# k and v loads over all 128 partitions, q halves on two queues, and the first batch's attention chain reordered with its last ninth deferred, in a linear attention + MLP kernel

## The chip, the cores and the metric

The kernel runs on one core of one Trainium2 chip. The metric is the time of one execution on the device in microseconds (us). Executions of one kernel mostly agree within 0.3 to 1%; where an execution was marked as slow (over 1.5% above the fastest of the same kernel), it is left out. The span of the profile is about 1.8 us shorter than the timed execution.

## The reference

```python
# q, k, v: [8 batches, 8 heads, 576 tokens, 64], float32
q_s = softmax(q, over the 64 columns)
k_s = softmax(k, over the 576 tokens)
kv  = einsum('bhsd,bhse->bhde', k_s, v)          # 64 x 64 per head
out = einsum('bhsd,bhde->bhse', q_s, kv)
x   = out with heads side by side                # 4608 tokens x 512
h   = x @ w_in                                   # 512 -> 2048
g   = max(0.01 * h, h)
return g @ w_out                                 # 2048 -> 512, float32
```

The work is dominated by the two products of the MLP: 9 tiles of 512 tokens, each with 64 matmuls of 128x512 for GEMM1 (`ph`) and 64 for GEMM2 (`pout`). One batch has 576 tokens, so a batch of attention gives one whole tile of 512 tokens and its last ninth (64 tokens) goes into the next tile.

## The kernel before

All of q, k and v arrive as halves of 64 partitions: one transfer for partitions 0 to 63, one for 64 to 127. A partition holds 9 consecutive tokens of a head, so each piece is 2304 bytes. Each half is 590 KB.

```python
def load(eng, dst, src_dram, b, nm, half):
    if nm == "q":
        src = src_dram[b, half * NG : (half + 1) * NG, :, :]      # heads 0-3 | 4-7
    else:
        src = src_dram[b].rearrange("(g hp) s d -> hp g s d", hp=2)[half]   # even | odd heads
    eng.dma_start(out=dst[half * HP : (half + 1) * HP, :, :],
                  in_=src.rearrange("h (p r) d -> p h (r d)", r=R))
...
for nm in "qkv":
    emit_load(nc.sync, states[0], 0, nm)          # first batch: six halves on SP's queue
...
# GpSimd's queue. The copy waits for the first batch's k: it holds back all that follows.
nc.gpsimd.tensor_copy(out=gate[HP:P, :], in_=states[0]["k"][HP:P, NG - 1, 0:1])
for i in range(WQ):
    emit_w_in(i)                                  # four quarters of w_in, cast to bf16 on the way
emit_load(nc.gpsimd, states[1], 1, "q")
emit_w_out(0)
emit_w_out(1)
emit_load(nc.gpsimd, states[1], 1, "k")
emit_w_out(2)
emit_load(nc.gpsimd, states[1], 1, "v")
emit_w_out(3)
for nm in "qkv":
    emit_load(nc.gpsimd, states[2], 2, nm)
```

The first batch's attention runs before the first tile of the MLP. `dummies` are matmuls with zero weights whose result nobody uses; they are there to keep TensorE's clock up. In the kernel before they also read the exponentials of q and k, so the first of them starts at 13.04 us. In the changed kernel they read the zero tile alone and start at 1.19 us.

```python
def first_attn(st):
    make_qexp(st, b, 0)(); make_qexp(st, b, 1)()      # ScalarE
    make_kexp(st, b, 0)(); make_kexp(st, b, 1)()      # ScalarE, one call per half
    make_qnorm(st, b, 0)()                            # VectorE: sum, reciprocal, multiply
    dummies(7, ...)
    make_transpose(st, b, [0], 0, R - 1, nc.scalar.copy)()
    make_qnorm(st, b, 1)()
    dummies(6, ...)
    make_vcast(st, b, 0, 2)(); make_vcast(st, b, 2, NG)()
    make_transpose(st, b, [1], 0, R - 1)()
    dummies(4, ...)
    make_kv(st, b, 0, 2)(); make_kv(st, b, 2, NG)()
    make_transpose(st, b, [0, 1], R - 1, R)()         # the last ninth
    for g in range(NG):
        make_out(st, b, g, copies[g % 2])()           # 512 and 64 tokens
```

During GEMM2 of the first tile (the loop runs over j = 0 to 15 outside, so w_out is needed quarter by quarter), the second batch's attention is prepared in slots: its k at j = 5, transposes at 6 to 8, v at 10, kv products at 12.

The softmax here doesn't subtract the row's maximum and nothing guards it: scores larger than these inputs give would overflow.

Of the kernel before, what the change touches and what calls it, by code (L numbers as in the profile page):

```python
# [18 lines left out]
def kernel(  # L19
# [50 lines left out]
    def load(eng, dst, src_dram, b, nm, half):  # L70
        if nm == "q":
            src = src_dram[b, half * NG : (half + 1) * NG, :, :]
        else:
            src = src_dram[b].rearrange("(g hp) s d -> hp g s d", hp=2)[half]
        eng.dma_start(  # L75
            out=dst[half * HP : (half + 1) * HP, :, :],
            in_=src.rearrange("h (p r) d -> p h (r d)", r=R),
        )

    dram = {"q": q, "k": k, "v": v}  # L80

    def emit_load(eng, st, b, nm):
        st[nm] = ld_pool.tile([P, NG, R * D], FP32, name=f"{nm}_ld", tag="ld")
        for half in range(2):
            load(eng, st[nm], dram[nm], b, nm, half)

    states = {b: {} for b in range(B)}
    for nm in "qkv":
        emit_load(nc.sync, states[0], 0, nm)
# [9 lines left out]
    for i in range(2):  # L99
# [4 lines left out]
        nc.vector.memset(ke[0:HP, :, :, HP:P], 0.0)  # L104
        nc.vector.memset(ke[HP:P, :, :, 0:HP], 0.0)
        nc.vector.memset(vb[:, :, :, D:VW], 1.0)
        nc.vector.memset(kd, 0.0)
# [3 lines left out]
        kd_buf.append(kd)  # L111

# [22 lines left out]
    nc.gpsimd.tensor_copy(out=gate[HP:P, :], in_=states[0]["k"][HP:P, NG - 1, 0:1])  # L135
    for i in range(WQ):
        emit_w_in(i)
    emit_load(nc.gpsimd, states[1], 1, "q")
    emit_w_out(0)
    emit_w_out(1)  # L140
    emit_load(nc.gpsimd, states[1], 1, "k")
    emit_w_out(2)
    emit_load(nc.gpsimd, states[1], 1, "v")
    emit_w_out(3)
    for nm in "qkv":
        emit_load(nc.gpsimd, states[2], 2, nm)
# [3 lines left out]
    def dummies(n, rhs):  # L150
        if "t" not in scratch:
            scratch["t"] = ps_pool.tile([P, TT], FP32, name="scr", tag=BANK)
        for _ in range(n):
            nc.tensor.matmul(scratch["t"], lhsT=wsrc[:, 0:P], rhs=rhs, start=True, stop=True)  # L154

    def flat(ap):
        return ap.rearrange("p a b -> p (a b)")
# [11 lines left out]
    def make_kexp(st, b, hp):  # L169
        def piece():  # L170
            lo = hp * HP
            nc.scalar.activation(  # L172
                out=ke_buf[b % 2][lo : lo + HP, :, :, lo : lo + HP],
                in_=st["k"][lo : lo + HP, :, :].rearrange("p g (r d) -> p g r d", d=D),
                func=AF.Exp,
            )

        return piece
# [10 lines left out]
    def make_qnorm(st, b, gl):  # L189
        def piece():  # L190
            x = qe_buf[b % 2][:, gl, :, :].rearrange("p r (h d) -> p (r h) d", d=D)
            qsum = small_pool.tile([P, 2 * R], FP32, name="qsum")
            qrec = small_pool.tile([P, 2 * R], FP32, name="qrec")
            nc.vector.reduce_sum(out=qsum, in_=x, axis=AX.X)  # L194
            nc.vector.reciprocal(out=qrec, in_=qsum)
# [3 lines left out]
                in1=qrec.unsqueeze(2).to_broadcast([P, 2 * R, D]),  # L199
# [64 lines left out]
    def make_out(st, b, g, big=None):  # L264
        def piece():
            t, o = divmod(b * S, TT)
            n1 = TT - o
            for c0, c1, tt, oo in ((0, n1, t, o), (n1, S, t + 1, 0)):
                po = ps_pool.tile([P, c1 - c0], FP32, name="po", tag=BANK)
# [3 lines left out]
                copy = nc.scalar.copy if c0 == 0 else nc.vector.tensor_copy  # L273
                if c0 == 0 and big is not None:
                    copy = big
                copy(out=xT_of(tt)[:, g, oo : oo + c1 - c0], in_=po)  # L276
# [3 lines left out]
    def prep_pieces(b, st):  # L280
# [5 lines left out]
            make_kexp(st, b, 0),  # L286
            make_kexp(st, b, 1),
# [11 lines left out]
    def out_pieces(b, st, copies=None):  # L299
        return [make_out(st, b, g, copies) for g in range(NG)]  # L300

    def first_attn(st):
        b = 0
        qe, ke = qe_buf[0], ke_buf[0]
        copies = (nc.scalar.copy, nc.vector.tensor_copy)
# [172 lines left out]
```

## Time and profile before

| | before |
|---|---|
| time, median (lowest to highest of 3) | 310.95 us (308.95 to 311.01) |
| span of the profile | 309.0 us |
| first matmul of GEMM1 | 24.42 us |
| first matmul of GEMM2, first tile | 38.23 us |
| first matmul of GEMM1, second tile | 63.59 us |
| from there to the end | 245.4 us |

From the second tile on, PE is busy nearly all the time. What can be won lies in the first 64 us.

The page cuts the span into 40 slices of 7.7 us; digits are busy tenths, PEclk is the granted TensorE clock in tenths. DMA and GB/s show what the 16 DMA engines did.

```profile
PE   0379994899999999999999999999999999999993
...
PEclk9999999599999999999999999999999999999998
DMA  7999999996996981699169917981400220121022
GB/s 163 222 211 224 222 225 224 226 234 172 221 210 164 224 176 34 160 217 185 34 159 220 188 34 160 224 178 34 105 0 2 68 68 0 36 68 34 2 68 68
```

The DMA engines are full from the start to about 60 us (the first eight slices), yet move only some 220 GB/s. PE is nearly idle in the first two slices, and the clock drops to half in one slice.

The next lines are from the timeline of the kernel before: start in us, duration, engine, source line, operation, output<-inputs, shapes, and in brackets how long the engine had been idle and what ended it.

```profile
8.74 2.21 ACT L161 ACTIVATE qe_102<-q_ld 128x1152 bf16<-128x1152 f32 x2 [6.50 <-DMA q_ld<-in_q_dram]
...
14.10 0.18 POOL L135 COPY gate<-k_ld 64x1 f32<-64x1 f32 x1 [12.79 <-DMA k_ld<-in_k_dram]
...
19.51 1.72 DVE L182 CAST vb_104<-v_ld 128x1152 bf16<-128x1152 f32 x2 [3.57 <-DMA v_ld<-in_v_dram]
...
24.42 13.98 PE L326 MATMUL ph<-xT,w_in_sb 128*128 128x512 bf16 x64
```

ScalarE waits 6.5 us for q, VectorE waits 3.6 us for v, GpSimd lets the weights go only at 14.1 us, and GEMM1 starts 4.9 us after v's cast begins. The times of the loads from issue to landing give 5.8 and 8.6 us for q, 11.3 and 14.0 for k, 16.6 and 19.4 for v: one half every 2.7 us, which is 590 KB / 2.7 us = 218 GB/s.

The second loss is in GEMM2 of the first tile (timeline of the kernel before, PE):

```profile
47.81 1.02 PE L335 MATMUL pout<-w_out_sb,g_sb 128*128 128x512 bf16 x4 [1.61 <-DMA w_out_sb<-in_moe_w_out_dram]
...
55.34 1.87 PE L335 MATMUL pout<-w_out_sb,g_sb 128*128 128x512 bf16 x4 [3.81 <-DMA w_out_sb<-in_moe_w_out_dram]
```

PE waits 1.6 and 3.8 us for quarters of w_out, and after the second wait four matmuls take 1.87 us instead of 1.02: this is the half clock.

### The profile page before, as it was taken

The numbers are of one execution on the slowest core, as the hardware profiler recorded it, in microseconds if no ns is written. First come the engines' busy times: TensorE is split into PE (matmuls) and PEld (weight loads), VectorE is DVE, ScalarE is ACT, GpSimd is POOL, SyncE is SP. The second block draws the span as 40 slices with busy tenths as digits, with TensorE's granted clock in tenths as the row PEclk, the third lists the DMA queues.
The fourth block names the chain that finished last, engine by engine and source line by source line (L and its number), as shares of the span: only waits on it lengthen the run. The fifth ranks groups of instructions, "written<-read, shape, count | busy, mean of one in ns | idle before, by whom it ended". The sixth has DMA issues, their size and how long they took to land.

```text
span 309.0 us, 4094 instructions
## 1 busy us (share of the span) xinstructions
PE 283.3 (92%) x1665; PEld 138.8 (45%) x1665; DVE 131.9 (43%) x235; ACT 142.4 (46%) x189; POOL 14.7 (5%) x27
## 2 busy tenths in 40 slices
PE   0379994899999999999999999999999999999993
PEld 0144452444545544554455445544544444444441
DVE  6653082337795609460946094609460100110021
ACT  1725761079663484358435833583343046006400
POOL 0171321000000000000000000000000000000000
PEclk9999999599999999999999999999999999999998
DMA  7999999996996981699169917981400220121022
GB/s 163 222 211 224 222 225 224 226 234 172 221 210 164 224 176 34 160 217 185 34 159 220 188 34 160 224 178 34 105 0 2 68 68 0 36 68 34 2 68 68
DMA packets 21522, 42.21 MB, mean 137 GB/s; under 512 B 2048, under 2 KB 6144, under 8 KB 21504
## 3 DMA queue, kind: packets, MB, share of 16 engines
q1 hardware_dynamic: 15552, 30.68, 45.3%
q0 software_dynamic: 5952, 11.27, 18.4%
q8 instruction: 13, 0.21, 0.3%
q14 instruction: 5, 0.04, 0.0%
HBM read 36.70 MB, written 9.44 MB: 149 GB/s over the span
## 4 chain that ended last, share of the span: by engine, by line
PE 78%; DMA 15%; ACT 2%; POOL 1%; issue 1%; SPq 1%; DVE 0%; POOLq 0%
PE pout L335 38%; PE ph L326 34%; DMA w_out_sb<-in_moe_w_out_dram 6%; DMA q_ld<-in_q_dram 6%; DMA k_ld<-in_k_dram 4%; PE pkv L238 3%; PE po L270 2%; PE pt L213 2%; ACT ke_103 L172 1%; POOL w_in_sb L123 1%; ACT g_sb L356 1%; SPq L75 1%; DVE out_sb L345 0%; POOL q_ld L75 0%; POOL gate L135 0%
## 5 line engine op out<-in xcount | busy, mean ns | idle before, releaser
L356 ACT ACTIVATE g_sb<-ph 128x512 bf16<-128x512 f32 x144 | 84.4, 597 | 111.7 <-PE ph L326 109.3
L335 PE MATMUL pout<-w_out_sb,g_sb 128*128 128x512 bf16 x576 | 129.1, 382 | 5.5 <-DMA w_out_sb<-in_moe_w_out_dram 5.4
L326 PE MATMUL ph<-xT,w_in_sb 128*128 128x512 bf16 x576 | 132.9, 379 | 0.0
L335 PEld LDWEIGHTS <-g_sb 128*128 128x128 bf16 x576 | 56.3, 98 | 72.4 <-issue 7.1
L326 PEld LDWEIGHTS <-w_in_sb 128*128 128x128 bf16 x576 | 54.9, 98 | 58.9 <-issue 0.2
L345 DVE COPY out_sb<-pout 128x512 f32<-128x512 f32 x36 | 24.3, 688 | 111.4 <-PE pout L335 104.8
L276 DVE CAST xT<-po 128x64 bf16<-128x64 f32 (+7 forms) x54 | 21.0, 425 | 7.1 <-PE po L270 6.5
L222 DVE COPY qT<-pt 128x128 bf16<-128x128 bf16 (+1 forms) x31 | 13.0, 447 | 14.2 <-PE pt L213 14.2
L172 ACT ACTIVATE ke_111<-k_ld 64x2304 bf16<-64x2304 f32 x8 | 16.9, 2118 | 2.7 <-DMA k_ld<-in_k_dram 2.7
L172 ACT ACTIVATE ke_103<-k_ld 64x2304 bf16<-64x2304 f32 x8 | 16.9, 2116 | 1.0 <-DMA k_ld<-in_k_dram 0.9
L194 DVE TENSOR_REDUCE qsum<-qe_110 128x18 f32<-128x1152 bf16 x8 | 10.8, 1350 | 13.7 <-ACT qe_110 L161 13.6
L276 ACT CAST xT<-po 128x448 bf16<-128x448 f32 (+2 forms) x10 | 4.8, 524 | 22.9 <-PE po L270 22.9
L154 PE MATMUL scr<-qe_102,wsrc 128*128 128x512 bf16 x7 | 3.2, 631 | 13.0 <-DVE qe_102 L196 13.0
L194 DVE TENSOR_REDUCE qsum<-qe_102 128x18 f32<-128x1152 bf16 x8 | 10.8, 1349 | 3.0 <-ACT qe_102 L161 2.9
L161 ACT ACTIVATE qe_102<-q_ld 128x1152 bf16<-128x1152 f32 x8 | 9.0, 1156 | 6.6 <-DMA q_ld<-in_q_dram 6.5
L196 DVE TENSOR_TENSOR qe_102<-qe_102,qrec 128x1152 bf16<-128x1152 bf16 x8 | 10.9, 1358 | 0.3
L196 DVE TENSOR_TENSOR qe_110<-qe_110,qrec 128x1152 bf16<-128x1152 bf16 x8 | 10.9, 1358 | 0.3
L161 ACT ACTIVATE qe_110<-q_ld 128x1152 bf16<-128x1152 f32 x8 | 9.0, 1155 | 2.1 <-DMA q_ld<-in_q_dram 2.0
L154 PEld LDWEIGHTS <-wsrc 128*128 128x128 bf16 x17 | 1.8, 115 | 15.1 <-DVE qe_102 L196 13.0
L246 DVE RECIPROCAL krec<-pkv 128x2 f32<-128x2 f32 x16 | 2.7, 169 | 12.6 <-PE pkv L238 12.5
L182 DVE CAST vb_104<-v_ld 128x2304 bf16<-128x2304 f32 (+1 forms) x5 | 5.8, 1171 | 3.6 <-DMA v_ld<-in_v_dram 3.6
L238 PEld LDWEIGHTS <-ke_111 128*128 128x128 bf16 x144 | 6.4, 107 | 2.0 <-issue 0.6
(40 smaller groups left out, 102.3 us busy)
## 6 DMA issues: line engine op xcount, KB each, us to landing
out_dram<-out_sb SPq DMA_DIRECT2D x72, 128.0 KB, 2.3
q_ld<-in_q_dram SPq DMA_DIRECT2D x12, 576.0 KB, 6.4
k_ld<-in_k_dram SPq DMA_DIRECT2D x12, 576.0 KB, 10.2
v_ld<-in_v_dram SPq DMA_DIRECT2D x12, 576.0 KB, 14.4
q_ld<-in_q_dram POOLq DMA_DIRECT2D x4, 576.0 KB, 18.6
k_ld<-in_k_dram POOLq DMA_DIRECT2D x4, 576.0 KB, 21.0
v_ld<-in_v_dram POOLq DMA_DIRECT2D x4, 576.0 KB, 20.0
w_in_sb<-in_moe_w_in_dram POOLq DMA_DIRECT2D x4, 512.0 KB, 9.4
```

Of the source, the lines that this page charges most:

```text
L161: nc.scalar.activation(out=qe_buf[b % 2][:, gl, :, :].rearrange("p r (h d) -> p h r d", d=D), in_=st["q"][:, 2 * gl : 2 * gl + 2, :].rearr ...
L172: nc.scalar.activation(out=ke_buf[b % 2][lo : lo + HP, :, :, lo : lo + HP], in_=st["k"][lo : lo + HP, :, :].rearrange("p g (r d) -> p g r ...
L194: nc.vector.reduce_sum(out=qsum, in_=x, axis=AX.X)
L196: nc.vector.tensor_tensor(out=x, in0=x, in1=qrec.unsqueeze(2).to_broadcast([P, 2 * R, D]), op=ALU.mult,)
L213: nc.tensor.matmul(pt[:, i, r - r0, :], lhsT=qe_buf[b % 2][:, gl, r, :], rhs=ident, is_transpose=True, start=(i == 0 and r == r0), stop=(i ...
L222: (copy or nc.vector.tensor_copy)(out=st["qT"][:, gl::2, r0 * HP : r1 * HP].rearrange("c gh (r p) -> c r gh p", p=HP), in_=pt[:, i, :, :]. ...
L238: nc.tensor.matmul(pkv[:, g - g0, 0 : D + 1], lhsT=ke[:, g, r, :], rhs=vb[:, g, r, 0 : D + 1], start=(r == 0), stop=(r == R - 1),)
L276: copy(out=xT_of(tt)[:, g, oo : oo + c1 - c0], in_=po)
L326: nc.tensor.matmul(ph, lhsT=w_in_sb[:, cb, j * P : (j + 1) * P], rhs=x[:, cb, :], start=(cb == 0), stop=(cb == NB - 1),)
L335: nc.tensor.matmul(pout, lhsT=g_sb[:, j, tsub * P : (tsub + 1) * P], rhs=w_out_sb[:, j, :], start=(j == 0), stop=(j == NF - 1),)
L345: nc.vector.tensor_copy(out=out_sb, in_=pout)
L356: nc.scalar.activation(out=g_sb[:, j, :], in_=ph, func=AF.Prelu, alpha=LEAKY_SLOPE)
```

## The change

The intent: move k and v in one transfer over all 128 partitions (in this layout partition p of group g is simply a contiguous run of memory), put the lower and upper half of q on two queues (SP and ScalarE) so that they move at the same time, let the first batch's exponentials and products start on parts of the data, and take work that the first tile does not need (the last ninth, the second set of memsets) out of the way of GEMM1. The core of the diff:

```diff
+    def load_q(eng, st, b, gh, h0, h1):
+        src = q[b, gh * NG + h0 : gh * NG + h1].rearrange("h (p r) d -> p h (r d)", r=R)
+        eng.dma_start(out=st["q"][gh * HP : (gh + 1) * HP, h0:h1, :], in_=src)
+
+    def load_kv(eng, st, b, nm, g0, g1):
+        flat = (k if nm == "k" else v)[b].rearrange("h s d -> (h s d)")
+        src = flat.rearrange("(g p f) -> p g f", g=NG, p=P)[:, g0:g1, :]
+        eng.dma_start(out=st[nm][:, g0:g1, :], in_=src)
...
-    for nm in "qkv":
-        emit_load(nc.sync, states[0], 0, nm)
+    for h0 in (0, 2):
+        load_q(nc.sync, states[0], 0, 0, h0, h0 + 2)
+        load_q(nc.scalar, states[0], 0, 1, h0, h0 + 2)
+    for nm in "kv":
+        for g0 in (0, 2):
+            load_kv(nc.sync, states[0], 0, nm, g0, g0 + 2)
...
-    emit_load(nc.gpsimd, states[1], 1, "q")
+    load_q(nc.gpsimd, states[1], 1, 0, 0, NG)          # lower half only
...
+    def load_q1_upper():                               # upper half: SP's queue, and only
+        nc.scalar.copy(out=states[1]["q"][HP:P, 0, 0:1], in_=wsrc[HP:P, 0:1])   # after this copy
+        load_q(nc.sync, states[1], 1, 1, 0, NG)
...
     def first_attn(st):
+        dummies(24)
         make_qexp(st, b, 0)()
         make_qexp(st, b, 1)()
+        make_kexp(st, b, 0, 2)()                       # by group pairs, not by halves
+        make_qnorm(st, b, 0, 0, R - 1)()               # eight ninths
+        make_qnorm(st, b, 1, 0, R - 1)()
+        make_transpose(st, b, [0], 0, R - 1, acopy)()
+        dummies(7)
+        make_kexp(st, b, 2, NG)()
+        make_vcast(st, b, 0, 2)()
+        make_transpose(st, b, [1], 0, R - 1, acopy)()
+        make_kv(st, b, 0, 2)()
+        make_vcast(st, b, 2, NG)()
+        dummies(2)
+        make_out(st, b, 0, TT, 0, dcopy)()             # 512 tokens only
+        make_out(st, b, 1, TT, 0, acopy)()
+        make_kv(st, b, 2, NG)()
+        make_out(st, b, 2, TT, 0, dcopy)()
+        make_out(st, b, 3, TT, 0, acopy)()
...
+            put((1, 4), [lambda: clear(1)])            # in GEMM1 of the first tile:
+            put((1, 5), [load_q1_upper])               # memsets, upper q of batch 1,
+            rest = first_attn_rest(states[0])          # and the last ninth
+            put((1, 4), rest[0:2])
+            put((1, 6), rest[2:3])
+            put((1, 7), rest[3:5])
+            put((1, 8), rest[5:7])
```

All later batches load q in two halves and k and v in one transfer each.

More of the change, by code (lines that the diff above doesn't have):

```diff
@@ L68, with new_ld @@
     ctx.enter_context(tc.manual_schedule())
-    def load(eng, dst, src_dram, b, nm, half):
-        if nm == "q":
-            src = src_dram[b, half * NG : (half + 1) * NG, :, :]
-        else:
-            src = src_dram[b].rearrange("(g hp) s d -> hp g s d", hp=2)[half]
-        eng.dma_start(
-            out=dst[half * HP : (half + 1) * HP, :, :],
-            in_=src.rearrange("h (p r) d -> p h (r d)", r=R),
-        )
-    dram = {"q": q, "k": k, "v": v}
-    def emit_load(eng, st, b, nm):
-        st[nm] = ld_pool.tile([P, NG, R * D], FP32, name=f"{nm}_ld", tag="ld")
-        for half in range(2):
-            load(eng, st[nm], dram[nm], b, nm, half)
+    def new_ld(st, nm):
+        st[nm] = ld_pool.tile([P, NG, R * D], FP32, name=f"{nm}_ld", tag="ld")
+    def load_q(eng, st, b, gh, h0, h1):
[5 more added lines that the diff above has]
+        eng.dma_start(out=st[nm][:, g0:g1, :], in_=src)
     states = {b: {} for b in range(B)}
     for nm in "qkv":
-        emit_load(nc.sync, states[0], 0, nm)
+        new_ld(states[0], nm)
+    for h0 in (0, 2):
[4 more added lines that the diff above has]
+            load_kv(nc.sync, states[0], 0, nm, g0, g0 + 2)
     wsrc = const_pool.tile([P, TT], BF16, name="wsrc")
@@ L103 @@
         kd = const_pool.tile([P, NG, P], BF16, name=f"kd{i}")
-        nc.vector.memset(ke[0:HP, :, :, HP:P], 0.0)
-        nc.vector.memset(ke[HP:P, :, :, 0:HP], 0.0)
-        nc.vector.memset(vb[:, :, :, D:VW], 1.0)
-        nc.vector.memset(kd, 0.0)
         qe_buf.append(qe)
@@ L111, with clear @@
         kd_buf.append(kd)
+    def clear(i):
+        nc.vector.memset(ke_buf[i][0:HP, :, :, HP:P], 0.0)
+        nc.vector.memset(ke_buf[i][HP:P, :, :, 0:HP], 0.0)
+        nc.vector.memset(v_buf[i][:, :, :, D:VW], 1.0)
+        nc.vector.memset(kd_buf[i], 0.0)
+    clear(0)
     w_in_sb = w_pool.tile([P, NB, F], BF16, name="w_in_sb")
@@ L134, with load_batch, dummies @@
     gate = const_pool.tile([P, 1], FP32, name="gate")
-    nc.gpsimd.tensor_copy(out=gate[HP:P, :], in_=states[0]["k"][HP:P, NG - 1, 0:1])
+    nc.gpsimd.tensor_copy(out=gate, in_=states[0]["k"][:, NG - 1, 0:1])
     for i in range(WQ):
         emit_w_in(i)
-    emit_load(nc.gpsimd, states[1], 1, "q")
+    for nm in "qkv":
+        new_ld(states[1], nm)
+    load_q(nc.gpsimd, states[1], 1, 0, 0, NG)
     emit_w_out(0)
     emit_w_out(1)
-    emit_load(nc.gpsimd, states[1], 1, "k")
+    load_kv(nc.gpsimd, states[1], 1, "k", 0, NG)
     emit_w_out(2)
-    emit_load(nc.gpsimd, states[1], 1, "v")
+    load_kv(nc.gpsimd, states[1], 1, "v", 0, NG)
     emit_w_out(3)
-    for nm in "qkv":
-        emit_load(nc.gpsimd, states[2], 2, nm)
+    def load_q1_upper():
+        nc.scalar.copy(out=states[1]["q"][HP:P, 0, 0:1], in_=wsrc[HP:P, 0:1])
+        load_q(nc.sync, states[1], 1, 1, 0, NG)
+    def load_batch(eng, b):
+        for nm in "qkv":
+            new_ld(states[b], nm)
+        for gh in range(2):
+            load_q(eng, states[b], b, gh, 0, NG)
+        for nm in "kv":
+            load_kv(eng, states[b], b, nm, 0, NG)
+    load_batch(nc.gpsimd, 2)
     scratch = {}
-    def dummies(n, rhs):
+    def dummies(n):
         if "t" not in scratch:
@@ L153, in dummies @@
         for _ in range(n):
-            nc.tensor.matmul(scratch["t"], lhsT=wsrc[:, 0:P], rhs=rhs, start=True, stop=True)
-    def flat(ap):
-        return ap.rearrange("p a b -> p (a b)")
+            nc.tensor.matmul(scratch["t"], lhsT=wsrc[:, 0:P], rhs=wsrc, start=True, stop=True)
     def make_qexp(st, b, gl):
@@ L167, in make_qexp, with make_kexp @@
         return piece
-    def make_kexp(st, b, hp):
+    def make_kexp(st, b, g0, g1):
         def piece():
-            lo = hp * HP
-            nc.scalar.activation(
-                out=ke_buf[b % 2][lo : lo + HP, :, :, lo : lo + HP],
-                in_=st["k"][lo : lo + HP, :, :].rearrange("p g (r d) -> p g r d", d=D),
-                func=AF.Exp,
-            )
+            for lo in (0, HP):
+                nc.scalar.activation(
+                    out=ke_buf[b % 2][lo : lo + HP, g0:g1, :, lo : lo + HP],
+                    in_=st["k"][lo : lo + HP, g0:g1, :].rearrange("p g (r d) -> p g r d", d=D),
+                    func=AF.Exp,
+                )
         return piece
@@ L187, in make_vcast, with make_qnorm @@
         return piece
-    def make_qnorm(st, b, gl):
+    def make_qnorm(st, b, gl, r0=0, r1=R):
         def piece():
-            x = qe_buf[b % 2][:, gl, :, :].rearrange("p r (h d) -> p (r h) d", d=D)
+            n = 2 * (r1 - r0)
+            x = qe_buf[b % 2][:, gl, r0:r1, :].rearrange("p r (h d) -> p (r h) d", d=D)
             qsum = small_pool.tile([P, 2 * R], FP32, name="qsum")
             qrec = small_pool.tile([P, 2 * R], FP32, name="qrec")
-            nc.vector.reduce_sum(out=qsum, in_=x, axis=AX.X)
-            nc.vector.reciprocal(out=qrec, in_=qsum)
+            nc.vector.reduce_sum(out=qsum[:, 0:n], in_=x, axis=AX.X)
+            nc.vector.reciprocal(out=qrec[:, 0:n], in_=qsum[:, 0:n])
             nc.vector.tensor_tensor(
@@ L198, in piece @@
                 in0=x,
-                in1=qrec.unsqueeze(2).to_broadcast([P, 2 * R, D]),
+                in1=qrec[:, 0:n].unsqueeze(2).to_broadcast([P, n, D]),
                 op=ALU.mult,
@@ L262, in xT_of, with make_out @@
         return xT[t]
-    def make_out(st, b, g, big=None):
+    def make_out(st, b, g, hi=S, lo=0, copy=None):
         def piece():
@@ L268, in piece @@
             for c0, c1, tt, oo in ((0, n1, t, o), (n1, S, t + 1, 0)):
+                if c0 >= hi or c1 <= lo:
+                    continue
                 po = ps_pool.tile([P, c1 - c0], FP32, name="po", tag=BANK)
@@ L272, in piece @@
                 )
-                copy = nc.scalar.copy if c0 == 0 else nc.vector.tensor_copy
-                if c0 == 0 and big is not None:
-                    copy = big
-                copy(out=xT_of(tt)[:, g, oo : oo + c1 - c0], in_=po)
+                cp = copy or (nc.scalar.copy if c0 == 0 else nc.vector.tensor_copy)
+                cp(out=xT_of(tt)[:, g, oo : oo + c1 - c0], in_=po)
         return piece
@@ L285, in prep_pieces @@
             make_qnorm(st, b, 1),
-            make_kexp(st, b, 0),
-            make_kexp(st, b, 1),
+            make_kexp(st, b, 0, 2),
+            make_kexp(st, b, 2, NG),
             make_vcast(st, b, 0, NG),
@@ L297, in kv_pieces, with out_pieces, first_attn_rest @@
         return [make_kv(st, b, 0, 2), make_kv(st, b, 2, NG)]
-    def out_pieces(b, st, copies=None):
-        return [make_out(st, b, g, copies) for g in range(NG)]
+    def out_pieces(b, st, copy=None):
+        return [make_out(st, b, g, copy=copy) for g in range(NG)]
     def first_attn(st):
         b = 0
-        qe, ke = qe_buf[0], ke_buf[0]
-        copies = (nc.scalar.copy, nc.vector.tensor_copy)
+        acopy, dcopy = nc.scalar.copy, nc.vector.tensor_copy
+        dummies(24)
         make_qexp(st, b, 0)()
         make_qexp(st, b, 1)()
-        make_kexp(st, b, 0)()
-        make_kexp(st, b, 1)()
-        make_qnorm(st, b, 0)()
-        dummies(7, flat(qe[:, 0, 0:4, :]))
-        make_transpose(st, b, [0], 0, R - 1, nc.scalar.copy)()
-        make_qnorm(st, b, 1)()
-        dummies(6, flat(ke[:, 0, 0:4, :]))
+        make_kexp(st, b, 0, 2)()
[4 more added lines that the diff above has]
+        make_kexp(st, b, 2, NG)()
         make_vcast(st, b, 0, 2)()
+        make_transpose(st, b, [1], 0, R - 1, acopy)()
+        make_kv(st, b, 0, 2)()
         make_vcast(st, b, 2, NG)()
-        make_transpose(st, b, [1], 0, R - 1)()
-        dummies(4, flat(ke[:, 0, 0:4, :]))
-        make_kv(st, b, 0, 2)()
+        dummies(2)
+        make_out(st, b, 0, TT, 0, dcopy)()
+        make_out(st, b, 1, TT, 0, acopy)()
         make_kv(st, b, 2, NG)()
-        make_transpose(st, b, [0, 1], R - 1, R)()
-        for g in range(NG):
-            make_out(st, b, g, copies[g % 2])()
+        make_out(st, b, 2, TT, 0, dcopy)()
+        make_out(st, b, 3, TT, 0, acopy)()
+    def first_attn_rest(st):
+        b = 0
+        pieces = [make_qnorm(st, b, 0, R - 1), make_qnorm(st, b, 1, R - 1)]
+        pieces += [make_transpose(st, b, [0, 1], R - 1, R)]
+        pieces += [make_out(st, b, g, S, TT, nc.vector.tensor_copy) for g in range(NG)]
+        return pieces
     def gemm1_mm(ph, x, j, cb):
@@ L444 @@
         if t > 0 and t + 2 < B:
-            for nm in "qkv":
-                emit_load(nc.sync, states[t + 2], t + 2, nm)
+            load_batch(nc.sync, t + 2)
         emit_moe(t, slots_of(t))
```

## The prediction

> **What bounds the kernel now.** From 24.4 us (first GEMM1 matmul, timeline) the kernel is bound by TensorE: the stretch table has PE busy in all but about 0.3 us after 62 us, and the last matmul ends at 304.3 of a 309.0 us span. What is not PE work lies in two places.
>
> 1. The start. First-batch transfers land at 5.8 and 8.6 (q), 11.3 and 14.0 (k), 16.6 and 19.5 us (v): 2.7 us per 590 KB half, 218 GB/s. Each half covers 64 partitions. The Trainium skill (SBUF — State Buffer, Door 1) says 64 partitions reach 8 of 16 ports, about 218 GB/s; the trace agrees: 2304-byte packets took 181 ns at the median, 91 at best, which over 16 engines is about 400 GB/s. The v cast waits for v (3.6 us, table of waits).
> 2. The w_out loads. DMA is full from 2 to about 55 us (slices). GEMM2 of the first tile waits 1.6 us at 46.2 and 3.8 us at 51.5 for w_out. After the second wait the clock is 0.5 for 6.8 us, worth about 3 us more. Total about 8.4 us.
>
> **What the change does.**
> - k and v over 128 partitions; q's halves together on two queues: estimated 1.5 us per 590 KB instead of 2.7. Estimated landings: q 4.7/6.2, k 7.6/9.1, v 10.6/12.1. The gate for the weights goes from 14.1 to about 9.3.
> - First chain: q exp 4.7-7.3, k exp of the first pair 7.6-10, norms on VectorE (2.7 us each) 6-11.4, first v cast to 12.4, first kv to 13.2, its scaling to 14.1, second v cast to 15.0, second kv to 15.9, scaling to 16.8, last two products to 17.3. GEMM1 starts at about 17.4 instead of 24.4: 7 us, all on the critical path.
> - The last ninth (two small norms, 2 transposes, 4 products of 64 columns) and the second set of memsets (2.6 us of VectorE) move under GEMM1: about 0.7 us of PE added there, waits hidden.
> - 24 early dummies warm the clock while PE is idle anyway: free.
> - DMA sequence after w_in[0] (21.4 to 55.3 us in before: 33.9 us): k1 and v1 save about 4.8, q1 up to 2.7. w_in[0] lands at about 14.7, w_out[0..3] at about 29.7, 32.4, 37.2, 42.2. GEMM2 starts at about 32 and needs them at 32, 35.3, 40, 43.5. So the two waits and the cold clock mostly go: 8.4 us, though margins are only 1 to 3 us.
> - Splitting k exp into four calls adds a few tenths of a us of ScalarE per batch, off the path.
>
> **Sum.** 310.95 - 7.0 - 8.4 + 0.7 = about 296.2; I say **296.5 us**, 80% range **293.5 to 301.5**. Chances: faster by over 2% **0.95**, within 2% **0.045**, slower **0.005**.
>
> **What would show it.** First GEMM1 matmul near 17.4; slices of the first 12 us near 350-400 GB/s instead of 220; v landed near 12; no PE wait on w_out of more than 1 us, granted clock near 1.0 between 30 and 70 us; PE about 272 us from first GEMM1 to the last matmul (279.9 before); steady tiles still 27.6 us plus attention.
>
> **What would make it wrong.** (a) The two q queues don't overlap, or 128-partition loads stay below 300 GB/s: start later by 2-4 us. (b) The first chain is then bound by VectorE/ScalarE in series, not by loads, so queueing there may cost 1-2 us. (c) GEMM2 catches up with the w_out loads: it starts 7 us earlier while the weight bytes are unchanged; a wait of over 3 us would cool the clock again and cost up to 5 us. (d) The second batch's upper q half comes late on its own queue and holds ScalarE in order before the last activation of the tile: 1-3 us.

## The result, and the profile after

The changed kernel takes 299.15 us (median of 4, 298.82 to 299.75) against 310.98 us for the kernel before beside it. The ratio is 0.9634 (95% interval 0.9588 to 0.968). Ratios here are fast runs against fast runs beside them, so they are not quite the ratio of the medians. The change gains 11.8 us; the prediction was a gain of 14.5.

| | before | after | difference |
|---|---|---|---|
| first matmul of GEMM1 | 24.42 | 18.73 | -5.7 |
| GEMM1 of the first tile lasts | 13.81 | 14.69 | +0.9 |
| GEMM2 of the first tile lasts | 25.36 | 19.58 | -5.8 |
| second tile to the end | 245.4 | 245.0 | -0.4 |
| span | 309.0 | 298.0 | -11.0 |

So all the gain is made before the second tile, half at the start and half in GEMM2 of the first tile. The 0.9 us in GEMM1 are the last ninth, now inside it, and a wait of 0.5 us at its end.

The slices of the changed kernel (each 7.4 us):

```profile
PE   8779997999999999999999999999999999999993
...
PEclk9999999999999999999999999999999999999998
DMA  7999999889069315941496139713101310130033
GB/s 173 335 203 214 310 301 221 344 177 355 25 153 290 133 35 119 272 192 35 109 210 268 35 83 200 300 35 71 38 2 35 70 35 2 39 85 17 2 70 70
```

PE is busy from the first slice (the early dummies). The clock has no half-speed slice any more. DMA reaches 335 GB/s in the second slice, but the first slice is at 173, hardly above the 163 of before. A table by stretches shows it better. Its columns are busy us and instruction counts by engine, granted clock, DMA share and GB/s. The kernel before:

```profile
core 0: us, PE busy (x) PEld busy (x) DVE busy (x) ACT busy (x) POOL busy (x), PEclk, DMA share, GB/s
...
2.00:8.00 6.00, 0.00 (x0) 0.00 (x0) 4.17 (x8) 0.23 (x2) 0.00 (x0) 1.00 0.97 221
8.00:14.00 6.00, 0.96 (x3) 0.41 (x4) 4.00 (x4) 4.35 (x4) 0.00 (x0) 1.00 1.06 224
...
33.00:41.00 8.00, 8.00 (x39) 3.63 (x37) 1.58 (x2) 6.28 (x9) 2.29 (x4) 1.00 1.17 222
41.00:48.00 7.00, 5.39 (x37) 2.88 (x36) 5.58 (x7) 4.24 (x2) 1.56 (x3) 1.00 1.12 226
```

The changed kernel:

```profile
2.00:8.00 6.00, 6.00 (x20) 2.34 (x19) 2.61 (x5) 2.65 (x3) 0.00 (x0) 1.00 0.97 237
8.00:14.00 6.00, 4.25 (x46) 2.37 (x45) 5.26 (x7) 5.45 (x5) 2.94 (x5) 1.00 1.02 365
...
33.00:41.00 8.00, 7.47 (x39) 3.49 (x40) 5.62 (x6) 5.02 (x5) 1.51 (x2) 1.00 1.12 335
41.00:48.00 7.00, 4.72 (x28) 2.44 (x30) 3.25 (x6) 2.33 (x3) 0.00 (x0) 1.00 1.12 248
```

From 2 to 8 us, when q is on its way, the two kernels move 221 and 237 GB/s: q is hardly faster. From 8 to 14 us, when k and v come, it is 224 and 365.

The same columns for the whole of GEMM2 of the first tile, first the kernel before, then the changed one:

```profile
38.23:63.59 25.36, 19.94 (x128) 10.29 (x127) 11.82 (x22) 8.84 (x9) 3.42 (x6) 0.87 1.09 227
...
33.42:53.00 19.58, 17.14 (x124) 8.92 (x128) 11.83 (x22) 9.28 (x11) 1.51 (x2) 1.00 1.09 286
```

GEMM2 is 5.8 us shorter: PE is busy 2.8 us less with the same work, which is what the half clock from 54.2 to 61.1 us cost in the profile of before, and idle 3.0 us less.

The timeline of the changed kernel, the lines that answer to those of before:

```profile
5.94 1.16 ACT L179 ACTIVATE qe_104<-q_ld 128x1152 bf16<-128x1152 f32 x1 [2.31 <-DMA q_ld<-in_q_dram]
...
8.49 1.16 ACT L179 ACTIVATE qe_104<-q_ld 128x1152 bf16<-128x1152 f32 x1 [1.39 <-DMA q_ld<-in_q_dram]
...
9.63 2.34 ACT L190 ACTIVATE ke_105<-k_ld 64x1152 bf16<-64x1152 f32 x2
...
11.05 0.18 POOL L142 COPY gate<-k_ld 128x1 f32<-128x1 f32 x1 [9.75 <-DMA k_ld<-in_k_dram]
...
11.99 1.01 ACT L241 COPY qT<-pt 128x1024 bf16<-128x1024 bf16 x1
12.49 0.91 DVE L200 CAST vb_106<-v_ld 128x1152 bf16<-128x1152 f32 x1
...
13.03 2.33 ACT L190 ACTIVATE ke_105<-k_ld 64x1152 bf16<-64x1152 f32 x2
...
15.38 1.01 ACT L241 COPY qT<-pt 128x1024 bf16<-128x1024 bf16 x1
...
16.45 0.38 PE L292 MATMUL po<-qT,kd_107 128*128 128x512 bf16 x1 [0.98 <-ACT qT L241]
16.45 0.82 PEld L257 LDWEIGHTS <-ke_105 128*128 128x128 bf16 x18 [1.27 <-issue]
...
18.73 6.21 PE L354 MATMUL ph<-xT,w_in_sb 128*128 128x512 bf16 x27
...
33.42 6.22 PE L363 MATMUL pout<-w_out_sb,g_sb 128*128 128x512 bf16 x27 [0.49 <-DMA w_out_sb<-in_moe_w_out_dram]
...
34.04 1.16 ACT L179 ACTIVATE qe_108<-q_ld 128x1152 bf16<-128x1152 f32 x1 [1.34 <-DMA q_ld<-in_q_dram]
...
47.40 1.02 PE L363 MATMUL pout<-w_out_sb,g_sb 128*128 128x512 bf16 x4 [1.84 <-DMA w_out_sb<-in_moe_w_out_dram]
```

q lands at 5.9 and 8.4 us. From 8.49 to 16.39 us ScalarE works without a pause (exp of q, exp of k, copy, exp of k, copy), and the second output product on PE waits for that last copy until 16.45. GEMM1 follows at 18.73. Then PE waits 0.5 us at 33.4 and 1.8 us at 47.4 for w_out, and ScalarE waits 1.3 us for q of the second batch. The landings, worked out from issue and time to landing: the four quarters of w_in at 17.5, 20.2, 23.7 and 27.4 us, those of w_out at 33.4, 35.8, 41.2 and 47.4. In the kernel before the first quarter of w_in landed at 21.4 and the last of w_out at 55.3.

### The profile page after: what moved, and what is told of

It is laid out like the page before. It is cut to its first block, busy times and chain, and to the rows that moved or that the text cites. A ratio compares the mean times of both kernels' runs of the same rounds, so it can differ in the third digit from the quotient of the medians.

```text
span 298.0 us, 4090 instructions
## 1 busy us (share of the span) xinstructions
PE 283.5 (95%) x1650; PEld 138.3 (46%) x1681; DVE 132.3 (44%) x240; ACT 147.0 (49%) x207; POOL 12.3 (4%) x22
## 4 chain that ended last, share of the span: by engine, by line
PE 82%; DMA 14%; SPq 1%; issue 1%; POOL 1%; DVE 0%
PE pout L363 38%; PE ph L354 37%; DMA w_out_sb<-in_moe_w_out_dram 8%; DMA w_in_sb<-in_moe_w_in_dram 4%; PE pkv L257 3%; DMA k_ld<-in_k_dram 3%; PE po L292 2%; PE pt L232 2%; SPq L77 1%; POOL w_in_sb L130 1%; DVE out_sb L373 0%; SPq L82 0%; POOL gate L142 0%
## 5 line engine op out<-in xcount | busy, mean ns | idle before, releaser
L363 PE MATMUL pout<-w_out_sb,g_sb 128*128 128x512 bf16 x560 | 126.4, 379 | 3.2 <-DMA w_out_sb<-in_moe_w_out_dram 2.3
L190 ACT ACTIVATE ke_109<-k_ld 64x1152 bf16<-64x1152 f32 x16 | 18.6, 1160 | 2.2 <-DMA k_ld<-in_k_dram 1.9
L241 DVE COPY qT<-pt 128x128 bf16<-128x128 bf16 (+1 forms) x30 | 12.3, 439 | 14.3 <-PE pt L232 14.3
L190 ACT ACTIVATE ke_105<-k_ld 64x1152 bf16<-64x1152 f32 x16 | 18.5, 1158 | 0.3
L213 DVE TENSOR_REDUCE qsum<-qe_108 128x18 f32<-128x1152 bf16 x8 | 10.8, 1350 | 8.1 <-ACT qe_108 L179 8.0
L213 DVE TENSOR_REDUCE qsum<-qe_104 128x18 f32<-128x1152 bf16 (+2 forms) x10 | 11.1, 1109 | 3.2 <-ACT qe_104 L179 3.0
L215 DVE TENSOR_TENSOR qe_104<-qe_104,qrec 128x1152 bf16<-128x1152 bf16 (+2 forms) x10 | 11.2, 1118 | 0.3
L175 PE MATMUL scr<-wsrc 128*128 128x512 bf16 x32 | 9.8, 471 | 1.2 <-DVE wsrc L95 1.2
L215 DVE TENSOR_TENSOR qe_108<-qe_108,qrec 128x1152 bf16<-128x1152 bf16 x8 | 10.9, 1358 | 0.3
L292 PE MATMUL po<-qT,kd_107 128*128 128x512 bf16 (+7 forms) x32 | 6.4, 287 | 2.3 <-DVE kd_107 L267 1.3
L232 PE MATMUL pt<-ident,qe_104 128*128 128x128 bf16 x72 | 5.6, 219 | 1.6 <-DVE qe_104 L215 1.6
L257 PEld LDWEIGHTS <-ke_105 128*128 128x128 bf16 x144 | 5.5, 97 | 2.8 <-issue 1.5
```

What stands on the lines that cost most here:

```text
L190: nc.scalar.activation(out=ke_buf[b % 2][lo : lo + HP, g0:g1, :, lo : lo + HP], in_=st["k"][lo : lo + HP, g0:g1, :].rearrange("p g (r d) - ...
L213: nc.vector.reduce_sum(out=qsum[:, 0:n], in_=x, axis=AX.X)
L215: nc.vector.tensor_tensor(out=x, in0=x, in1=qrec[:, 0:n].unsqueeze(2).to_broadcast([P, n, D]), op=ALU.mult,)
L241: (copy or nc.vector.tensor_copy)(out=st["qT"][:, gl::2, r0 * HP : r1 * HP].rearrange("c gh (r p) -> c r gh p", p=HP), in_=pt[:, i, :, :]. ...
L257: nc.tensor.matmul(pkv[:, g - g0, 0 : D + 1], lhsT=ke[:, g, r, :], rhs=vb[:, g, r, 0 : D + 1], start=(r == 0), stop=(r == R - 1),)
L292: nc.tensor.matmul(po, lhsT=kd_buf[b % 2][:, g, :], rhs=st["qT"][:, g, c0:c1], start=True, stop=True)
```

## The experiments

Theory A at this point: the gain comes from k and v at full rate; from about 2 us to the last quarter of w_out the transfers are back to back and decide when the first tile can end, so the start of GEMM1 has some slack; q on two queues does nothing. Theory B: the reordered chain and the earlier start of GEMM1 count one for one. All runs gave correct results unless said otherwise. "Clock" is the mean granted clock of the fast runs; it does not count the time before the clock first goes up.

| run | time, median of all runs (us) | ratio to before | first GEMM1 | second tile | clock |
|---|---|---|---|---|---|
| after_again | 299.98 | 0.9677 (0.9645 to 0.9709) | 18.64 | 52.35 | 0.993 to 0.999 |
| q_one_queue | 300.52 | 0.9656 (0.9607 to 0.9705) | 19.54 | 55.05 | 0.991 to 0.997 |
| q_flat_b0 | 297.68 | 0.9599 (0.9561 to 0.9637) | 18.05 | 50.99 | 0.990 to 1.000 |
| q_flat_b01 | 297.66 | 0.9602 (0.9559 to 0.9645) | 17.43 | 49.27 | 0.988 to 1.000 |
| kv_halves_b0 | 304.73 | 0.9802 (0.9759 to 0.9846) | 22.98 | 54.63 | 0.981 to 0.994 |
| kv_halves_b1 | 305.24 | 0.9823 (0.9799 to 0.9847) | 18.99 | 56.58 | 0.974 to 0.994 |
| loads_only | 300.47 | 0.9683 (0.9665 to 0.9700) | 22.53 | 53.79 | 0.998 to 1.000 |
| no_defer | 303.78 | 0.9791 (0.9771 to 0.9811) | 21.78 | 57.29 | 0.987 to 0.989 |
| no_defer_early_q1 | 301.39 | 0.9717 (0.9691 to 0.9743) | 22.35 | 55.86 | 0.983 to 0.988 |
| warm_kv1 | 298.57 | 0.9624 (0.9598 to 0.9650) | 17.99 | 51.78 | 0.997 to 1.000 |
| no_dummies | 302.22 | 0.9733 (0.9705 to 0.9761) | 19.96 | 56.03 | 0.996 to 1.000 |
| best_all | 298.75 | 0.9616 (0.9589 to 0.9643) | 18.57 | 53.13 | 0.991 to 0.999 |

"First GEMM1" and "second tile" are the first matmuls in us of the one profiled execution, which need not be the median one. In every profile the time from the second tile to the end is 244.6 to 245.4 us, so in the profiles the second tile's start is the whole story. Times of clock changes are on the same time axis as the timelines.

### The changed kernel again

> The changed kernel again, as the yardstick for the runs beside it. Both theories: 298.8 to 299.8 us, ratio to before 0.959 to 0.968, first GEMM1 matmul at 18.7 us, last quarter of w_out landing at 47.4 us.

Measured: 299.98 us (299.07 to 300.85), ratio 0.9677: a little above the first measurement (0.9634); the intervals overlap. First GEMM1 at 18.64 us and last quarter of w_out at 46.7 us in this profile. Differences of under half a per cent between the runs below cannot be told apart.

### q on one queue

```diff
-        load_q(nc.scalar, states[0], 0, 1, h0, h0 + 2)
+        load_q(nc.sync, states[0], 0, 1, h0, h0 + 2)
```

> All four quarter loads of the first batch's q on the one SP queue, in the order lower, upper, lower, upper. Theory A (the two queues take turns in whole transfers on the same 16 engines[...]): q still lands at about 5.9 and 8.4 us (within 0.4), first GEMM1 matmul within 0.5 us of 18.7, time within 1 us of the changed kernel. Rival B (the two queues overlap in part and are worth something): q lands 1 us or more later, first GEMM1 at 19.5 or later, time 0.8 us or more longer.

Measured: 300.52 us and ratio 0.9656 against 0.9677, no difference; one of its six runs was slow and is left out of the ratio. In the profile q's first two quarters are there at 6.2 us and the last at 8.9 instead of 8.4. The nine profiles with q on two queues have the last quarter at 8.2 to 9.4 us, so 8.9 lies among them. First GEMM1 is at 19.54, which is B's number: 0.4 us of the delay is there at the second output product (16.89 instead of 16.45), the rest comes with a half clock from 18.8 to 22.2 us, which makes this one of the kernel's longer runs (301.8). A holds for the landings and the time; that profile cannot judge the start of GEMM1.

The packet records of the changed kernel, in quarter microseconds, show two things. Where both queues have q to move, they mostly pass one transfer after the other: at 5.0 and 5.25 us the ScalarE queue moves 258 and 286 GB/s and the SP queue 0 and 9. At the edges both move: 166 and 175 GB/s at 3.5, 92 and 120 at 4.5. And packets of 2304 bytes take 93 to 105 ns up to 4.25 us, also where both queues move, and mostly 160 to 175 ns after that. This is not an effect of the meeting: on one queue they are fast at first too (to about 4.0 us in this run, to 3.5 in the kernel before) and slow then (135 to 176 ns here; 182 at the median of the kernel before's first loads). Why the first half megabyte or so is fast stays open. After that first part the trace agrees with the Trainium skill (DMA: Bandwidth & Descriptors, "Rules for kernel authors"): two transfers to disjoint partition halves serialize, also from two queues, and one transfer over 128 partitions should be used instead. The prediction leaned on the ports and passed over that rule.

### q over 128 partitions, the first batch, then also the second (wrong results on purpose)

```diff
-        load_q(nc.sync, states[0], 0, 0, h0, h0 + 2)
-        load_q(nc.scalar, states[0], 0, 1, h0, h0 + 2)
+        load_kv(nc.sync, states[0], 0, "q", h0, h0 + 2)     # heads end up in wrong places
# second run, in addition:
-    load_q(nc.gpsimd, states[1], 1, 0, 0, NG)
+    load_kv(nc.gpsimd, states[1], 1, "q", 0, NG)
-        load_q(nc.sync, states[1], 1, 1, 0, NG)             # upper half and its trigger taken out
```

Heads land in places where the rest of the kernel does not expect them. The comparison with the reference did not flag this: q is 0.1 times noise, its softmax over 64 columns is nearly flat, and so a wrong head changes the result little. That these two runs passed means nothing; they are measurements of time only.

> Wrong result on purpose: the first batch's q is loaded over all 128 partitions at once like k and v (heads end up in wrong places), two transfers of 590 KB. Theory A (q at half rate is the term that the prediction mis-sized, and transfers are back to back up to the last quarter of w_out): q lands at about 4.2 and 5.6 us, everything behind it 2.8 us earlier, first GEMM1 matmul at about 16.7, last quarter of w_out at 44.6, time 2 to 3 us shorter than the changed kernel: about 296.5. Rival B (ScalarE and VectorE in series set the start, whatever q does): first GEMM1 above 18.2 and time within 0.7 us of the changed kernel.

Measured for the first batch alone (one of six runs, 301.70 us, was slow and is left out of the ratio): q lands at 4.5 and 5.8 us, as the prediction had hoped for two queues (4.7 and 6.2). Ratio 0.9599 against 0.9677: 0.8% or 2.4 us less, with intervals that do not overlap. So A's size is right. Not all of A's path is: k landed at 8.5 instead of about 7, the first GEMM1 was 0.6 us earlier and not 2, in a profile with the clock at half from 16.9 to 20.3 us; the last quarter of w_out landed at 45.4 instead of 46.7 to 47.4.

> Wrong result on purpose: as the run before, and the second batch's q too is one transfer over 128 partitions, on the GpSimd queue, none on SP. Theory A: a further 2 to 2.7 us less of transfers ahead of w_out, last quarter of w_out landing near 42, waits of PE on w_out under 0.7 us in all, time 1 to 2 us below the run with the first batch alone: about 295. Rival B: no further gain (within 0.5 us), since q of the second batch is not what w_out waits for.

Measured for both: the last quarter of w_out at 43.6 us, the wait for it 0.7 us, second tile at 49.27 in the profile, 3.1 to 3.7 us before the changed kernel's. But the ratio, 0.9602, is no better than for the first batch alone: the runs spread from 295.83 (clock 1.000) to 299.19 (clock 0.990). The last landing came 1.7 us before that of the run above, where A said 2 to 2.7; the time that should follow is not shown. The three runs over 298 us have clocks of 0.988 to 0.991, but so has the run at 297.01 (0.991); the two under 296.5 have 0.996 and 1.000.

### k and v in halves again, for one batch at a time

```diff
-        eng.dma_start(out=st[nm][:, g0:g1, :], in_=src)
+        for lo, hi in ((0, HP), (HP, P)) if b == 0 else ((0, P),):     # or b == 1
+            eng.dma_start(out=st[nm][lo:hi, g0:g1, :], in_=src[lo:hi])
```

> The changed kernel with the first batch's k and v again as two transfers of 64 partitions each. Theory A (loads at half rate are what the change removed): k lands at about 11.1 and 13.8, v at about 16.5 and 19.3 us, first GEMM1 at about 22.4 (3.7 later), last quarter of w_out about 5 us later at 52.4; time 5 us longer[...]: 304 to 307. Rival B (the reordered chain is what made the start earlier): first GEMM1 by 20.5, time below 302.

Measured: 304.73 us, 4 to 5 us longer. First GEMM1 at 22.98, as A expected (22.4), not by 20.5 as B did. The transfers cost less than expected, though: pieces of 295 KB landed every 1.2 us (243 GB/s), v was complete at 18.8, and the last quarter of w_out landed at 49.0, not 52.4; PE did not wait for it. Four of the six runs had a clock of 0.981 or 0.982; the profiled one, the fastest, had half clock from 14.5 to 21.4 us. In this profile the second tile comes only 1.6 to 2.3 us later than in the changed kernel's; what the other runs lost besides was not seen in a profile.

> The changed kernel with only the second batch's k and v as two transfers of 64 partitions each. Theory A: first GEMM1 unchanged at 18.7; transfers between the second and the last quarter of w_out take about 5 us longer, w_out ends at about 52.4; PE waits for w_out 6 to 7 us in all instead of 2.3, and the clock drops to half for several us after it: time 5 to 8 us longer, 304 to 307. Rival B (what counts is the start; w_out has slack): time within 1 us of the changed kernel.

Measured: 305.24 us (two of six runs slow and left out of the ratio; the median of the four fast ones is 304.64), 4 to 5 us longer, with the first GEMM1 unchanged at 18.99 us. B falls: the second batch's loads, far behind the start, count fully. The last quarter of w_out landed at 50.9 us. PE's wait for it was 2.1 us, less than A's 6 to 7, because PE already came late: ScalarE waited 2.8 us for the second batch's q, PE's transposes behind it 2.4 us, and the clock was at half from 18.8 to 22.2.

### k and v over 128 partitions and nothing else

The kernel before, with this alone (and the copy that releases GpSimd's queue reads k over all partitions):

```diff
     def emit_load(eng, st, b, nm):
         st[nm] = ld_pool.tile(...)
+        if nm != "q":
+            flat_src = dram[nm][b].rearrange("h s d -> (h s d)")
+            eng.dma_start(out=st[nm], in_=flat_src.rearrange("(g p f) -> p g f", g=NG, p=P))
+            return
```

> The kernel before, with nothing of the change but k and v over 128 partitions (its chain, its q loads and its memsets as they were). Theory A: v lands at about 14.4 us, first GEMM1 at about 20.8, last quarter of w_out near 47.5, and since w_out decides, the time is within 1.5 us of the changed kernel: 299 to 301. Rival B (new chain, dummies and deferred ninth are worth about half of the gain): 302.5 to 306.

Measured: 300.47 us (300.22 to 300.84), ratio 0.9683, against 0.9677 for the whole change in its own rounds. This is the main result. The loads of k and v alone take 3.2% off the time, the whole change 3.2% and 3.7% in its two measurements; whether the rest of it is worth up to half a per cent is not resolved. The rest of the change without the k and v loads was not run. Its PE timeline:

```profile
22.53 13.98 PE L332 MATMUL ph<-xT,w_in_sb 128*128 128x512 bf16 x64
36.34 6.21 PE L341 MATMUL pout<-w_out_sb,g_sb 128*128 128x512 bf16 x28
...
48.20 1.02 PE L341 MATMUL pout<-w_out_sb,g_sb 128*128 128x512 bf16 x4 [0.33 <-DMA w_out_sb<-in_moe_w_out_dram]
...
53.79 2.54 PE L332 MATMUL ph<-xT,w_in_sb 128*128 128x512 bf16 x11
```

GEMM1 starts at 22.53 us, 3.8 to 3.9 us later than in the two profiles of the changed kernel. Yet GEMM2 waits only 0.3 us for w_out, and the second tile starts at 53.79, against 53.00 and 52.35 there. The rest of the change moves the start by 3.8 to 3.9 us, and 2.5 to 3.0 us of that are given back before the second tile, 1.5 to 2.0 of them as longer waits for w_out. B falls. First GEMM1 came 1.7 us later than A's 20.8, since this start no longer waited for v: v landed at 14.6, but VectorE had the norms of q ahead of it in the program and began v's cast at 15.88; PE had idle matmuls and transposes ahead and began the kv products at 19.07, although the cast had ended at 17.40:

```profile
15.88 1.52 DVE L188 CAST vb<-v_ld 128x1152 bf16<-128x1152 f32 x2
...
19.07 1.31 PE L244 MATMUL pkv<-vb,ke 128*128 128x65 bf16 x36
```

### The last ninth before GEMM1 again

```diff
         make_out(st, b, 3, TT, 0, acopy)()
+        for piece in first_attn_rest(st):
+            piece()
# and the slots that ran it inside GEMM1 taken out
```

> The changed kernel with the last ninth of the first batch's attention done before GEMM1 again. Theory A (the last quarter of w_out decides, the start of GEMM1 has about 2.3 us of slack): first GEMM1 about 2 us later (20.5 to 21), the waits for w_out shrink by as much, time within 0.7 us of the changed kernel. Rival B (the start of GEMM1 counts one for one): time about 2 us longer.

Measured: 303.78 us (303.37 to 304.50), nearly 4 us longer. Both theories fail: A expected nothing, B two. The first GEMM1 was 3.1 us later and the second tile 4.9. ScalarE's timeline shows one reason:

```profile
40.34 1.16 ACT L179 ACTIVATE qe<-q_ld 128x1152 bf16<-128x1152 f32 x1 [3.48 <-DMA q_ld<-in_q_dram]
```

The upper q half of the second batch starts only after the sixth activation of GEMM1. With GEMM1 late, that copy ran at 29.2 us instead of 24.8. ScalarE had this activation next in its program, so it stood for 3.5 us, and PE's transposes then waited 1.6 and 1.5 us. The second reason is the clock: it was at half from 21.1 to 24.5 us (an earlier stretch, 10.8 to 14.3, cost nothing visible: the second output product came at 16.42, as in the changed kernel), and all four runs had a mean of 0.987 to 0.989, against 0.993 to 0.999 for the changed kernel. So the start of GEMM1 has slack against w_out, but two other things are tied to it.

> The run without the deferral (303.8 us) again, but the load of the second batch's upper q half is started right after the first attention chain, not after the sixth activation of GEMM1. Theory A2 (the 4 us of that run came mostly from this load: its start is tied to GEMM1's progress, it landed 6 us later, ScalarE stood in order behind it for 3.5 us and the transposes of the second batch came late; the rest is half clock in GEMM1): ScalarE waits under 1 us for the q load, GEMM2 of the first tile takes 17.3 to 19 us instead of 20.4, time 300 to 302. Rival B2 (later GEMM1 start counts one for one): first GEMM1 still about 21.8 and time still above 303.

The edit was the one above, plus:

```diff
-            put((1, 5), [load_q1_upper])
     first_attn(states[0])
+    load_q1_upper()
```

Measured: 301.39 us, 2.4 us less than the run above. First GEMM1 is still late (22.35), ScalarE no longer waits for q, and GEMM2 lasts 16.96 us instead of 20.36, with the last quarter of w_out at 45.5. So A2 holds, B2 falls. Much of what is left of the loss is in GEMM1, which lasts 16.55 us where 14 is normal, at half clock from 21.1 to 27.9 us.

### The order before GEMM1, and more idle matmuls

```diff
-        dummies(2)
+        dummies(3)
         make_out(st, b, 0, TT, 0, dcopy)()
-        make_out(st, b, 1, TT, 0, acopy)()
+        dummies(1)
         make_kv(st, b, 2, NG)()
+        make_out(st, b, 1, TT, 0, acopy)()
+        dummies(3)
         make_out(st, b, 2, TT, 0, dcopy)()
```

> The changed kernel with the second kv product ahead of the second output product on PE, and seven idle matmuls in the gaps just before GEMM1 instead of two. Theory A (the start of GEMM1 has slack before the last quarter of w_out; half clock in GEMM1, seen in some executions, is the part of the spread that counts): first GEMM1 about 17.9 instead of 18.7, no 0.5 clock between 10 us and the end, and yet the median within 1 us of the changed kernel (298.5 to 300), with a longer wait for w_out. Rival B (start counts): 0.8 us or more shorter than the fastest runs of the changed kernel, so below 298.3.

Measured: 298.57 us (298.11 to 299.83). First GEMM1 at 17.99 us, clock 0.997 or more in all six runs. The waits for w_out:

```profile
PE pout L365 <- DMA w_out_sb<-in_moe_w_out_dram: 2.2, 2, 1.2
```

They stayed at 2.2 us in all, and the second tile started at 51.78. The median is within A's range (298.5 to 300) and not below 298.3, but only just. In the profile the start is 0.65 to 0.74 us earlier than in the two of the changed kernel and the second tile 0.6 to 1.2 us earlier, and the waits did not grow as A said, so this run does not separate A and B. The ratio 0.9624 is below 0.9677 of the changed kernel in its second measurement and like 0.9634 in its first, so a gain over the changed kernel is possible (up to half a per cent) and not shown.

### No idle matmuls

```diff
-        dummies(24)
-        dummies(7)
-        dummies(2)
```

> The changed kernel with none of the idle matmuls (24, 7 and 2 taken out). If they do their work (keeping the clock up for the chain and GEMM1): the clock is 0.5 until about 22 us, the kv products and the first 3.4 us or so of GEMM1 run at half speed, GEMM1 ends 1.5 to 3 us later; with the slack before w_out absorbing part, time 300 to 302. If the slack absorbs all: within 0.7 us of the changed kernel.

Measured: 302.22 us, 2 to 3 us longer. The clock goes up only at 24.2 us (6.2 in the changed kernel), GEMM1 starts at 19.96 and lasts 16.1 us, ScalarE later waits 3.05 us for the second batch's q (the same tie as above), and PE does not wait for w_out. So the idle matmuls earn 2 to 3 us in this kernel, as the first of the two expectations has it.

### A version put together

The edit is that of the run with the reordered kv product, the early start of the upper q half, and:

```diff
-    load_kv(nc.gpsimd, states[1], 1, "v", 0, NG)
     emit_w_out(3)
+    load_kv(nc.gpsimd, states[1], 1, "v", 0, NG)
...
-            put((2, 10), prep[6:7])          # cast of v
+            put((2, 12), prep[6:7])
-            put((2, 12), kv)
+            put((2, 14), kv)
-                put((2, 13 + i // 2), outs[i : i + 1])
+                put((2, 15), outs[i : i + 1])
```

> A version put together from what the runs before showed: the kv product first and seven idle matmuls in the gaps before GEMM1 (as the run before), the second batch's upper q half started right after the first attention chain, and the last quarter of w_out loaded ahead of the second batch's v, with the second batch's kv and output products moved back to the end of GEMM2. Theory A (after the k and v change, the first tile ends when the transfers allow it): first GEMM1 about 18.0, PE waits for w_out under 0.7 us in all, first matmul of the second tile at 50.5 to 51.5 instead of 52.4 to 53.0, time 296.5 to 298.5, beating the changed kernel by 0.3 to 0.9 per cent. Rival (the transfers saved there come back as a wait for v): second tile at 52 or later, 299 or more.

Measured: 298.75 us (297.99 to 299.93), ratio 0.9616. The last quarter of w_out now lands at 42.8 us and PE does not wait for it. But v lands at 48.1, 5.3 us after it and not about 2.7, and PE waits for its cast (PE timeline):

```profile
49.54 1.31 PE L257 MATMUL pkv<-vb,ke 128*128 128x65 bf16 x36 [2.81 <-DVE vb L200]
```

The wait has changed its name, from w_out to v, and the second tile starts at 53.13: the rival had that right. The median of 298.75 lies between A's 298.5 and the rival's 299, so neither has the time. v came late as its packets, at 178 ns until 43.8 us, then took about 350 to 440: that is when the half-partition transfers of the third batch's q, next in the queue, begin on the engines that are done. The records do not tell the two transfers' packets apart, so this last step is an inference. Both put-together versions are the fastest correct ones measured, by an amount over the changed kernel that is not resolved.

## Why the prediction was right or wrong, point by point

- **Time.** 299.15 us lies in the range (293.5 to 301.5), 2.7 us above the point.
- **k and v over 128 partitions, 1.5 us per 590 KB: right.** They landed at 9.6, 11.0, 12.4 and 13.9 us, 1.4 us apart, 416 GB/s. The Trainium skill (SBUF — State Buffer, Door 1) gives 8 of 16 ports for 64 partitions and about 218 GB/s; halves one after the other measured 218 here, and full transfers nearly twice that.
- **"q's halves together on two queues": wrong.** Predicted landings 4.7 and 6.2; measured 5.9 and 8.4. The two queues do not add up, and one queue does about as well (run q_one_queue). 590 KB of q are there at 5.9 us in the kernel before too, and all of it at 8.6, against 8.4. What brought ScalarE's start forward, from 8.7 to 5.9 us, is that q now comes in quarters, so that it can start when two of them are there. The run with q over 128 partitions got the predicted landings and 2.4 us: this is the largest mis-sized term that a run measured.
- **"GEMM1 starts at about 17.4: 7 us, all on the critical path": the size 5.7 us, and "all on the critical path" wrong.** The later q held up ScalarE, whose work without a pause to 16.4 us set the second output product (risk b of the prediction). And 22.5 us is early enough (run loads_only): of the 5.7 us, 1.9 came with the k and v loads alone, and the other 3.8 were mostly given back.
- **"8.4 us" of waits and cold (half) clock: 5.9 us; the waits shrank from 5.4 to 2.3 us, not to nothing.** The sum added two gains that compete: GEMM2 was to start 6 us earlier and also find its weights in time. The last quarter of w_out was predicted for 42.2 and landed at 47.4: 2.8 us because the first quarter of w_in came at 17.5 instead of 14.7 (the gate opened 1.8 us late, as k queued behind q), and 2.3 us because the stretch from there to w_out's end was 29.8 us instead of 27.5. This is risk (c); the longest wait was 1.8 us, and the clock stayed up after it. Where the start moved by 1.9 us only (run loads_only), GEMM2 got 7.9 us shorter, close to the 8.4: 5.1 of waits and 2.8 of half clock.
- **The half clock "worth about 3 us": right in the profile, not visible from run to run.** In GEMM2 of the first tile PE is busy 19.94 us before, 17.14 in the changed kernel and 17.12 in loads_only, for the same work: 2.8 us. But of the kernel before's 42 timed runs beside the experiments, the 16 with a mean clock of 0.987 or less have a median of 310.25 us and the 16 with 0.993 or more 310.03, and one with 1.000 took 310.02. The mean leaves out the time before the clock first goes up and says nothing of where a low stretch fell, so why these runs are no faster stays open.
- **Early dummies "free": right, and idle matmuls are needed** (run no_dummies, which took out all 33: 2 to 3 us). What the prediction missed is that the new chain leaves PE with little to do just before GEMM1. In the second measurement of the changed kernel the six runs' mean clocks spread from 0.993 to 0.999, and several variants' profiles show 3.4 us of half clock there.
- **Risk (d), the late upper q half, is real.** In the changed kernel ScalarE waited 1.3 us for it; when GEMM1 comes later it costs more (no_defer, no_dummies).
- **Steady tiles unchanged: right,** 245.4 and 245.0 us from the second tile on.

Open are: why the half clock of the kernel before does not show in its timed runs, how much of the 0.5% spread of the changed kernel is the half clock before GEMM1, why q over 128 partitions in the second batch brought earlier landings but no shorter times, and whether the third batch's q is why v took 5.3 us in the last run.

## What to carry to other kernels

Look at how many partitions a transfer covers before anything else: a load over 64 partitions ran at about half the rate (218 against 416 GB/s), two queues did not mend it, and one view of the same memory over 128 partitions gave by itself nearly all that it gave together with a rework of the chain behind it. Before adding up two gains, ask whether the first one makes the second harder: an earlier consumer meets the same transfers, and the start that a rework wins comes back as a wait unless the transfers move too. When a step is taken out or put in, check which loads are triggered by the progress of the step, for such a tie can cost more than the step.

## What the Trainium skill lacked or had wrong

- DMA: Bandwidth & Descriptors says that two half-partition transfers serialize, packet-interleaved if from two queues. Here the turns could be long (from 5.0 to 5.5 us nearly all came from one of the two queues). No page has packet times for the two kinds of transfer: 2304-byte packets took 93 to 100 ns over 128 partitions and about 170 to 190 ns over 64, from one queue as from two, except in the first 1.5 to 2.3 us of loading, when they took about 93 ns over 64 too.
- The same page does not say what a half-partition transfer does to its neighbours in the queue. In the last run packets went from 178 ns to about 350 to 440 ns when the next batch's q halves were due (an inference, see there).
- TensorE: Matmul & The Clock Gate, in its table of the two states, ties the low clock to an idle window of about 3.4 us. It also tells of a kernel whose clock dropped from frequent short idle times, but not how much idle time that takes. Half-clock stretches of 3.4 and 6.8 us agree with the window. But the drop at 21.1 us in the run no_defer came without such a pause: PE's longest idle time in the 3.4 us before was 1.4 us, with PE busy 0.94 of these 3.41 us.
